# Attention and two mixtures of experts on one core: VectorE, TensorE and a fourth row buffer take over small steps at the start of the routed experts

## The chip, the cores and the metric

The kernel runs on one core of a Trainium2 chip. The time is that of one execution on the device, in microseconds (us), and the figure of a kernel is the median of several executions. One execution is also recorded by the hardware profiler; its rows are what this text reads. TensorE is called PE in the rows (PEld is its loading of weights), VectorE is DVE, ScalarE is ACT, GpSimd is POOL, and SP is the queue from which most transfers are issued.

## The reference

Three layers follow each other. First attention in chunks of 32 positions (batch 4, 8 heads, 768 positions, 64 columns a head), where each chunk also looks at 8 memory rows. Then a soft mixture of 8 experts with 4 slots each. Then a mixture of 8 experts in which every row goes to the 2 experts with the largest noisy logits:

```
scores = scale * q_c @ concat(mem_k, k_ctx).T      # per chunk of 32
x = softmax(scores) @ concat(mem_v, v_ctx)         # 3072 rows of 512
d, c = softmax(x @ phi, axis=0), softmax(x @ phi, axis=1)
x = c @ [relu((d.T @ x)[e] @ w1[e]) @ w2[e] for e in range(8)]
noisy = x @ w_gate + log1p(exp(x @ w_noise)) * noise
top2 = the two largest of noisy in each row, weights = softmax of the two
out[r] += weight * (relu(x[r] @ w1[e]) @ w2[e])    # for both experts e of row r
```

There are 3072 rows, the inner width of every expert is 1024, and the two weight matrices of one expert are 2 MB each.

## The kernel before, in words

The order of the work on each engine is the order of the program text; nothing is reordered. Each engine takes its own instructions strictly in that order and waits where an operand isn't ready.

`attention` runs over 32 half units (a pair of heads and half a sequence). In each, `qk` makes scores in PSUM: three matrix products of 128 query columns against the 16 memory columns (line 1063), then twelve of 32 query columns each against the chunk's keys, four of them side by side in the column groups of the array (line 1070). `spread` (line 1035) copies the values that `load_v` brings. `soft` then streams the 16 weight matrices of the soft experts.

`experts` does the routed experts. Its rows are sorted by expert into tiles of 128 rows, 48 tiles in the usual case and one of leftovers; the first six tiles belong to expert 0 ("rank 0"), whose weights are loaded first. A tile goes through `gather` (GpSimd fetches 128 rows from a table in memory by the indices `idx`), `ct` (TensorE turns them), `l1` (first layer on TensorE, line 707; ScalarE takes the positive part into fp16, line 709, and `lo` on VectorE takes what that lost, line 717), `l2` (24 matrix products, line 741: high part times high weights, high part times low weights, low part times high weights), `gate` and `yv` (ScalarE scales the row into a buffer `y`, line 759) and `put` (two accumulating scatters from GpSimd, line 772).

Before the first tile of an expert, its weights are prepared. `prep_g` folds the soft layer's output into the first matrix; `prep_gmax` and `prep_max` (line 374) or `bound` (ScalarE, line 449) find the largest magnitudes; `prep_row` and `prep_all` spread the maximum over the partitions by two small TensorE transpositions with a VectorE maximum between them (lines 385 to 391), for ranks 1 to 7. For rank 0 `prep_par` does that on GpSimd in one instruction (line 381). `prep_s` makes the scales, `prep_hi` (ScalarE, line 427) and `prep_lo` (VectorE, line 431) split the second matrix, in four parts, into a high and a low fp16 half; the fourth low part of rank 0 is made by `prep_lop` on GpSimd (lines 436 and 437).

Where each row of the sorted order comes from is found in two steps. For the first six tiles `spread_s` builds a one-hot matrix from 24 compares (six and six by VectorE, five by GpSimd on line 544, the rest by ScalarE), `inverse` multiplies it out and `finish_idx` turns the result into indices. For all the others `bases` and `positions` (lines 608 to 620 and `split_pos`, lines 530 to 532) find the rows' places, `tiles` makes two masks (VectorE on line 814, then GpSimd on line 815), `spread_s` makes 32 compares on VectorE and 16 on ScalarE, and `inverse` and `finish_idx` follow in the loop. `order0` and `order1` (to line 601) rank the experts by size.

The text before the loop orders the first six tiles by hand. The loop then goes over n, with tile n's second layer, tile n+1's first layer and tile n+2's turning in step n; `PLAN` and `MID` add the preparation of the next expert to fixed steps. For rank 1 these are `prep_row` in step 2 ahead of that step's second layer, `prep_s`, `prep_gs` and the first part of the split in step 3, and the other three parts in step 4. `tile_tables` (to line 799) runs on VectorE in step 3, and step n also copies the first matrix of tile n+2 into one of two small buffers (`gcopy`, line 696). The second `inverse` with `finish_idx` and the gathers of tiles 6 to 9 stand at the end of step 2. Row buffers `y` rotate over three.

Of the kernel before, what the change touches and what calls it, by code (L numbers as in the profile page):

```python
# [27 lines left out]
F = 1024  # L28
# [82 lines left out]
def tile_kernel(ctx, tc, q, k, v, mem_k, mem_v, phi, sw1, sw2, wg, wn, noise, mw1, mw2, cf_in, c16_in, out):  # L111
# [12 lines left out]
    with ExitStack() as sctx:  # L124
# [48 lines left out]
        nc.gpsimd.dma_start(nz, noise.rearrange("(t p) e -> p t e", p=128))  # L173
        C = mid.tile([128, NT, SL], F32, name="C")
        CT = mid.tile([128, 6, 128], F32, name="CT")
        SOT = mid.tile([128, 4, SL], F32, name="SOT")
# [28 lines left out]
    with ExitStack() as ectx:  # L205
        rt = ectx.enter_context(tc.tile_pool(name="rt", bufs=1))
        ew = ectx.enter_context(tc.tile_pool(name="ew", bufs=2))
        ps = ectx.enter_context(tc.tile_pool(name="ps3", bufs=1, space=PSUM))
        experts(tc, nc, C, CT, SOT, sog, wgn, nz, zt, table, mw1, mw2, out, K, K16, rw, rt, ew, ps)

# [95 lines left out]

def experts(tc, nc, C, CT, SOT, sog, wgn, nz, zt, table, mw1, mw2, out, K, K16, rw, rt, ew, ps):
    idx = rt.tile([128, NSL], I32, name="idx")
# [70 lines left out]

    def prep_par(rk, a=0, b=2):  # L380
        nc.gpsimd.partition_all_reduce(sc[:, rk, 2 + a:2 + b], sc[:, rk, a:b], 128, bass.bass_isa.ReduceOp.absmax)

    def prep_row(rk):
# [9 lines left out]
    def prep_s(rk, a=0, b=2):  # L393
        ga = sc[:, rk, 2:4]
        src = RW.get((rk, "b"), ga)
        for x in range(a, b):
            ts(ga[:, x:x + 1], src[:, x:x + 1], (2.0 ** -10, 2.0 ** -13)[x], 1.0e-34, op0=OP.mult, op1=OP.max)
        gi = ga[:, a:b].bitcast(I32)
        ts(gi, gi, 0x7F800000, None, op0=OP.bitwise_and)
        nc.vector.reciprocal(sc[:, rk, 4 + a:4 + b], ga[:, a:b])  # L400
# [28 lines left out]
    def prep_lo(rk, part):  # L429
        w2, hi, lo = w2p(rk, part)  # L430
        stt(lo, w2, sc[:, rk, 5:6], hi, op0=OP.mult, op1=OP.subtract)  # L431

    def prep_lop(rk, part):
        w2, hi, lo = w2p(rk, part)
        t = W2r[:, 7 * 4096 + 3072:8 * 4096]
        nc.gpsimd.tensor_tensor(t, w2, bc(sc[:, rk, 5:6], 1024), OP.mult)
        nc.gpsimd.tensor_tensor(lo, t, hi, OP.subtract)

# [75 lines left out]
    vt(sc[:, 0, 1:2], s4[:, :4], AX.X, OP.max)  # L514
    prep_par(0)
    cc = T(2, dt=F16)
    nc.vector.tensor_copy(cc[:96], pc)
    pp = ps.tile([128, 192], F32, name="l1", bufs=2)
    for c in range(2):
        nc.tensor.matmul(pp, cc[:96, c:c + 1].to_broadcast([96, 128]), K16["m"][:96, 192 * c:192 * c + 192],  # L520
                         start=c == 0, stop=False)
    nc.tensor.matmul(pp, K16["u"], ohb, start=False, stop=True)
    ppe = pp.rearrange("p (t e) -> p t e", e=E)
    val0 = T(NT)
# [159 lines left out]
    GT = {}  # L684
    gbuf = [x.rearrange("p a b -> p (a b)").bitcast(F16)[:, :F] for x in (C, CT)]

# [67 lines left out]

    YV = {}

    def yv(i):
        YV[i] = ew.tile([128, DM], F32, name="y", bufs=3)
        nc.scalar.activation(YV[i], P2.pop(i), AF.Copy, scale=GW.pop(i))  # L759
# [74 lines left out]
    prep_hi(0, 2)  # L834
    bases()
    ns, tq = positions()
    gcopy(0)
# [9 lines left out]
    ts(gw0, gw0, sc[:, 0, 6:7], 2.0 ** -10, op0=OP.mult, op1=OP.mult)  # L847
    prep_lop(0, 3)
    wide_w()
    tiles(0)  # L850
    prep_lo(0, 0)
    tiles(1)
    l2(0, (0,), 2)
    l1(1, False)
    l2(0, (1,), 2)
    lo(1)
    prep_lo(0, 1)
    prep_lo(0, 2)
    load_e(1, 1)
    nc.sync.dma_start(table[0:N, 64:ROW].rearrange("(t p) c -> p t c", p=128), wd)  # L860
    spread_s(oh_s, ns, J2[0], J2[1], J2[2][:16])
    l2(1, (0, 1), 2)
    prep_g(1)
    ct(2)
    l2(0, (2,), 2)
    l1(2)
    gate(0)
    yv(0)
    spread_s(oh_s, ns, [], [], J2[2][16:])
    prep_max(1, 0, 2)  # L870
    bound(2)
    ct(3)
    bound(3)
    join_max(1)
    put(0)
    PLAN, MID = {}, {}
# [31 lines left out]
    for n, i in enumerate(seq):  # L908
# [28 lines left out]
        if n == 1:  # L937
            put(i)
        if n == 2:
            inverse(oh_s, o2, [*J2[2], *J2[1], *J2[0]], T0, NSL)  # L940
            pv2 = T(NSL - T0)
            nc.scalar.activation(pv2, pvs[T0], AF.Copy)
            pvs[T0] = pv2
            finish_idx(T0, NSL)
            for x in range(6, 9):
                gather(x)
            put(i)
            gather(9)
        if n > 2:
            put(i)  # L950
# [15 lines left out]
def attention(tc, nc, q, k, v, mem_k, mem_v, phi, xs, L, K, phis, arena, ab, wk, ps, load_piece):  # L966
# [89 lines left out]
    def qk(i):  # L1056
# [4 lines left out]
        for g in range(3):  # L1061
            t = 128 * (3 * s + g)
            nc.tensor.matmul(st[:, g, :, 28:32], QT[u][:, t:t + 128], MK[:, hp, b].rearrange("p h z m -> p (h z) m"),  # L1063
                             start=True, stop=True)
        for g in range(3):
            for j in range(4):
                c = 12 * s + 4 * g + j
                w0 = 8 if c == 0 else 0
                w1 = 24 if c == NCH - 1 else 28
                nc.tensor.matmul(st[32 * j:32 * j + 32, g, :, w0:w1], QT[u][:, 32 * c:32 * c + 32],  # L1070
                                 kb[:, :, 16 * c + w0:16 * c + w1], start=True, stop=True,
                                 tile_position=(0, 32 * j))
# [295 lines left out]
```

## Time and profile before

| what | value |
|---|---|
| time, median of three executions | 607.39 us (605.48 to 607.93) |
| the profiled execution: its time | 604.92 us |
| the profiled execution: its span, first to last instruction | 603.1 us |
| granted TensorE clock, mean over the span | 0.935 |
| busy: PE, DVE, ACT, POOL | 512.6, 331.2, 292.0, 290.0 us |
| transfers | 127.28 MB, mean 211 GB/s |

Some 1.8 us of the profiled time lie outside its span. Attention takes the span's first 175 us or so, the soft experts the stretch to 230 us, the start of the routed experts that to 315 us, and from there to 583 us TensorE runs tile after tile; what is left is the last scatters. A busy share is a mean over these stages, so what a change is worth has to be read from the stage in which it lies.

### The profile page before, as it was taken

The numbers are of one execution on the slowest core, as the hardware profiler recorded it, in microseconds if no ns is written. First come the engines' busy times: TensorE is split into PE (matmuls) and PEld (weight loads), VectorE is DVE, ScalarE is ACT, GpSimd is POOL, SyncE is SP. The second block draws the span as 40 slices with busy tenths as digits, with TensorE's granted clock in tenths as the row PEclk, the third lists the DMA queues.
The fourth block names the chain that finished last, engine by engine and source line by source line (L and its number), as shares of the span: only waits on it lengthen the run. The fifth ranks groups of instructions, "written<-read, shape, count | busy, mean of one in ns | idle before, by whom it ended". The sixth has DMA issues, their size and how long they took to land.

```text
span 603.1 us, 14142 instructions
## 1 busy us (share of the span) xinstructions
PE 512.6 (85%) x4859; PEld 294.6 (49%) x4859; DVE 331.2 (55%) x826; ACT 292.0 (48%) x510; POOL 290.0 (48%) x261
## 2 busy tenths in 40 slices
PE   3998798889888866266789989999999999999960
PEld 3886686766644323132344544544545455544520
DVE  5476667565774104499486574756647566352200
ACT  4798788877531203453372452635436272452310
POOL 6032223222003000386375766757767777877762
PEclk9999999999699978568799989999999999999995
DMA  9899999999999999955749698787978867546552
GB/s 183 204 223 210 215 226 266 229 221 261 226 404 363 413 411 355 323 173 145 176 86 293 135 241 230 179 209 160 248 218 215 215 151 191 81 84 103 85 65 26
DMA packets 99505, 127.28 MB, mean 211 GB/s; under 512 B 19238, under 2 KB 68026, under 8 KB 99434
## 3 DMA queue, kind: packets, MB, share of 16 engines
q1 hardware_dynamic: 79866, 109.30, 61.0%
q0 software_dynamic: 19152, 16.89, 20.9%
q8 instruction: 45, 0.74, 0.5%
q10 hardware_dynamic: 416, 0.15, 0.1%
q14 instruction: 26, 0.21, 0.1%
HBM read 94.84 MB, written 20.42 MB: 191 GB/s over the span
## 4 chain that ended last, share of the span: by engine, by line
PE 38%; DVE 5%; DMA 5%; issue 4%; ACT 2%; POOL 2%; SPq 0%; POOLq 0%; DVEq 0%; ACTq 0%
PE l L741 31%; DMA out_dram<-y,idx 3%; PE l L707 3%; PE g L362 2%; POOL out_dram L772 1%; DMA C<-G 1%; PE l L738 1%; ACT hi L709 1%; DVE lo L717 1%; DVE mxp L374 1%; DMA w<-in_moe_w_dram 1%; ACT W L427 1%; DVE G L414 1%; DVE W L814 1%; DVE W L431 0%
## 5 line engine op out<-in xcount | busy, mean ns | idle before, releaser
L772 POOL DMA_INDIRECT out_dram<-y,idx x96 | 155.0, 1614 | 78.8 <-DMA out_dram<-y,idx 40.5
L741 PE MATMUL l<-W,hi 128*128 (+1 forms) x768 | 180.1, 389 | 0.3 <-ACT hi L709 0.3
L717 DVE SCALAR_TENSOR_TENSOR lo<-l,hi 128x1024 f16<-128x1024 f32 x49 | 59.9, 1223 | 105.3 <-ACT hi L709 73.5
L741 PEld LDWEIGHTS <-hi 128*128 128x128 f16 x768 | 74.6, 100 | 86.1 <-issue 9.6
L759 ACT ACTIVATE y<-l,gw 128x512 f32<-128x512 f32 x49 | 33.5, 684 | 148.9 <-PE l L741 87.3
L741 PE MATMUL l<-W,lo 128*128 (+1 forms) x384 | 91.9, 383 | 5.5 <-DVE lo L717 5.5
L1024 POOL DMA_DIRECT2D arena<-in_mem_v_dram x64 | 39.3, 615 | 110.4 <-PE av L1113 86.9
L666 POOL DMA_INDIRECT cg<-table,idx x49 | 52.9, 1079 | 20.4 <-issue 13.4
L741 PEld LDWEIGHTS <-lo 128*128 128x128 f16 x384 | 37.1, 98 | 50.0 <-DVE lo L717 6.2
L709 ACT ACTIVATE hi<-l 128x1024 f16<-128x1024 f32 x49 | 50.2, 1024 | 10.2 <-PE l L707 8.7
L431 DVE SCALAR_TENSOR_TENSOR W<-w,sc,W 128x1024 f16<-128x1024 f32 x31 | 42.3, 1391 | 0.2
L1035 DVE COPY arena<-arena 32x768 f32<-32x768 f32 x32 | 17.8, 555 | 39.2 <-DMA arena<-in_v_dram 34.5
L1045 PE MATMUL tr<-cf,arena 128*128 128x128 f32 x192 | 32.0, 310 | 7.0 <-DMA arena<-in_q_dram 7.0
L1052 ACT ACTIVATE qT<-tr 64x384 f32<-64x384 f32 x64 | 33.3, 520 | 6.9 <-PE tr L1045 5.8
L427 ACT ACTIVATE W<-w,sc 128x1024 f16<-128x1024 f32 x32 | 35.7, 1149 | 0.2
L1052 ACT ACTIVATE arena<-tr 64x384 f32<-64x384 f32 x64 | 30.9, 483 | 4.9 <-PE tr L1045 4.1
L1113 PE MATMUL av<-arena,aT 128*32 128x130 f32 x768 | 30.1, 291 | 2.4 <-ACT aT L1104 2.1
L1070 PE MATMUL st<-arena,qT 128*32 128x112 f32 (+2 forms) x768 | 28.2, 282 | 4.7 <-ACT arena L1052 3.9
L1045 PEld LDWEIGHTS tr<-cf,arena 128*128 128x128 f32 x192 | 23.5, 156 | 12.7 <-issue 6.9
L374 DVE TENSOR_REDUCE mxp<-w 128x1 f32<-128x2048 f32 x13 | 29.6, 2275 | 0.0
L1063 PEld LDWEIGHTS st<-arena,qT 128*128 128x128 f32 x192 | 27.3, 214 | 2.2 <-issue 2.2
L1063 PE MATMUL st<-arena,qT 128*128 128x16 f32 x192 | 26.7, 266 | 1.5 <-issue 1.5
(270 smaller groups left out, 683.6 us busy)
## 6 DMA issues: line engine op xcount, KB each, us to landing
w<-in_moe_w_dram SPq DMA_DIRECT2D x88, 512.0 KB
arena<-in_moe_w_dram SPq DMA_DIRECT2D x28, 512.0 KB
arena<-in_v_dram SPq DMA_DIRECT2D x62, 168.0 KB
arena<-in_q_dram SPq DMA_DIRECT2D x16, 384.0 KB
arena<-in_k_dram SPq DMA_DIRECT2D x16, 384.0 KB
xs<-in_moe_w_dram SPq DMA_DIRECT2D x12, 512.0 KB
out_dram<-zt SPq DMA_DIRECT2D x14, 384.0 KB
C<-G SPq DMA_DIRECT2D x21, 256.0 KB
```

The costliest lines, as they stand in the source:

```text
L374: vt(t, w2[:, part * n:(part + 1) * n], AX.X, OP.max, apply_absolute_value=True)
L427: nc.scalar.activation(hi, w2, AF.Copy, scale=sc[:, rk, 5:6])
L431: stt(lo, w2, sc[:, rk, 5:6], hi, op0=OP.mult, op1=OP.subtract)
L666: nc.gpsimd.indirect_dma_start(out=CG[i], out_offset=None, in_=table, in_offset=bass.IndirectOffsetOnAxis(ap=idx[:, i:i + 1], axis=0))
L709: nc.scalar.activation(HI[i], p, AF.Relu)
L717: stt(LO[i].rearrange("p k t -> p (k t)"), p.rearrange("p k t -> p (k t)"), 0.0, HI[i].rearrange("p k t -> p (k t)"), op0=OP.max, op1=OP.s ...
L741: nc.tensor.matmul(P2[i], h[i][:, k, :], dyn(W2f, i, w * 4096 + 512 * k, 512, RG.get(i)), start=x == 0 and k == 0, stop=x == last and k == 7)
L772: nc.gpsimd.indirect_dma_start(out=o, out_offset=bass.IndirectOffsetOnAxis(ap=idx[:, i:i + 1], axis=0), in_=y[:, DH * h:DH * h + DH], in_o ...
L1024: nc.gpsimd.dma_start(vcols(i, p + 28, 4, col, 128), bass.AP(tensor=mem_v.tensor, offset=mem_v.offset + (b * H + 2 * hp + h) * NMEM * D, a ...
L1045: nc.tensor.transpose(p[:, T, :], src[:, h, T, :], identf)
L1052: nc.scalar.activation(o, i, AF.Copy)
L1063: nc.tensor.matmul(st[:, g, :, 28:32], QT[u][:, t:t + 128], MK[:, hp, b].rearrange("p h z m -> p (h z) m"), start=True, stop=True)
```

## The change

Five things are altered. `prep_par` is taken away, and rank 0 uses `prep_row` and `prep_all` like the other ranks. `prep_lop` is taken away, and all four low parts of rank 0 are made by VectorE: two right after `order1`, the other two among the low parts of tiles 0 and 1; `bases` and `positions` move behind them. The rest of the hand-written order is changed with that: `tiles`, rank 1's `prep_g` and the compares come after tile 2's first layer, `put(0)` comes earlier, and the second `inverse`, with its indices and the gathers of tiles 6 to 9, moves from the end of step 2 to the end of step 3. In attention, the memory's scores are made by twelve products of 32 query columns in the four column groups in place of three of 128. Last, the two tiles `C` and `CT` become one tile `CC`; the two small first-matrix buffers use its first two thirds, and the last third is a fourth row buffer.

```diff
@@ attention, qk
         for g in range(3):
-            t = 128 * (3 * s + g)
-            nc.tensor.matmul(st[:, g, :, 28:32], QT[u][:, t:t + 128], MK[:, hp, b].rearrange("p h z m -> p (h z) m"),
-                             start=True, stop=True)
-        for g in range(3):
+            for j in range(4):
+                c = 12 * s + 4 * g + j
+                nc.tensor.matmul(st[32 * j:32 * j + 32, g, :, 28:32], QT[u][:, 32 * c:32 * c + 32],
+                                 MK[:, hp, b].rearrange("p h z m -> p (h z) m"), start=True, stop=True,
+                                 tile_position=(0, 32 * j))
             for j in range(4):
@@ experts, maxima of rank 0
-    def prep_par(rk, a=0, b=2):
-        nc.gpsimd.partition_all_reduce(sc[:, rk, 2 + a:2 + b], sc[:, rk, a:b], 128, bass.bass_isa.ReduceOp.absmax)
...
     vt(sc[:, 0, 1:2], s4[:, :4], AX.X, OP.max)
-    prep_par(0)
     cc = T(2, dt=F16)
     nc.vector.tensor_copy(cc[:96], pc)
+    prep_row(0)
     pp = ps.tile([128, 192], F32, name="l1", bufs=2)
...
     nc.tensor.matmul(pp, K16["u"], ohb, start=False, stop=True)
+    prep_all(0)
@@ experts, buffers
-    gbuf = [x.rearrange("p a b -> p (a b)").bitcast(F16)[:, :F] for x in (C, CT)]
+    gbuf = [CC[:, x * F // 2:(x + 1) * F // 2].bitcast(F16) for x in range(2)]
...
-        YV[i] = ew.tile([128, DM], F32, name="y", bufs=3)
+        YV[i] = CC[:, F:F + DM] if YN[0] % 4 == 3 else ew.tile([128, DM], F32, name="y", bufs=3)
+        YN[0] += 1
@@ experts, the order ahead of the loop
     ct(0)
     prep_hi(0, 2)
-    bases()
-    ns, tq = positions()
+    prep_lo(0, 0)
+    prep_lo(0, 1)
...
     ts(gw0, gw0, sc[:, 0, 6:7], 2.0 ** -10, op0=OP.mult, op1=OP.mult)
-    prep_lop(0, 3)
-    wide_w()
-    tiles(0)
-    prep_lo(0, 0)
-    tiles(1)
     l2(0, (0,), 2)
     l1(1, False)
     l2(0, (1,), 2)
+    prep_lo(0, 2)
     lo(1)
-    prep_lo(0, 1)
-    prep_lo(0, 2)
+    prep_lo(0, 3)
     load_e(1, 1)
+    bases()
+    ns, tq = positions()
+    wide_w()
     nc.sync.dma_start(table[0:N, 64:ROW].rearrange("(t p) c -> p t c", p=128), wd)
-    spread_s(oh_s, ns, J2[0], J2[1], J2[2][:16])
-    l2(1, (0, 1), 2)
-    prep_g(1)
-    ct(2)
     l2(0, (2,), 2)
-    l1(2)
     gate(0)
     yv(0)
+    put(0)
+    ct(2)
+    l2(1, (0, 1), 2)
+    l1(2)
+    tiles(0)
+    tiles(1)
+    prep_g(1)
+    spread_s(oh_s, ns, J2[0], J2[1], J2[2][:16])
+    ct(3)
     spread_s(oh_s, ns, [], [], J2[2][16:])
     prep_max(1, 0, 2)
     bound(2)
-    ct(3)
     bound(3)
     join_max(1)
-    put(0)
@@ experts, the loop
-        if n == 2:
+        if n == 3:
             inverse(oh_s, o2, [*J2[2], *J2[1], *J2[0]], T0, NSL)
...
-        if n > 2:
+        elif n > 1:
             put(i)
```

## Rows read from the trace of the kernel before

**Rows 1.** The page's chain that ended last: shares of the span by engine.

```profile
PE 38%; DVE 5%; DMA 5%; issue 4%; ACT 2%; POOL 2%; SPq 0%; POOLq 0%; DVEq 0%; ACTq 0%
```

**Rows 2.** Stretches: from:to, length, busy us by engine (instructions), PE clock, DMA share, GB/s.

```profile
80.00:120.00 40.00, 36.23 (x604) 28.84 (x600) 26.12 (x70) 33.56 (x62) 10.39 (x18) 1.00 1.08 242
...
290.00:297.00 7.00, 6.41 (x17) 2.21 (x17) 1.78 (x6) 0.00 (x0) 2.36 (x2) 0.55 0.89 273
...
520.00:580.00 60.00, 59.89 (x344) 29.77 (x343) 22.90 (x56) 24.46 (x39) 45.49 (x32) 1.00 0.51 83
```

**Rows 3.** Timeline from 241 to 260 us: start, us, engine, line, operation [idle before].

```profile
241.81 0.37 POOL L381 PARTITION_ALL_REDUCE sc<-sc  x1 [11.40 <-DVE W L517]
...
242.71 0.18 DVE L531 SCALAR_TENSOR_TENSOR W<-W,l 128x24 f32<-128x24 f32 x1
...
245.08 1.05 DVE L546 TENSOR_SCALAR W<-c,W 128x128 f16<-128x128 f16 x6
...
249.91 2.93 POOL L544 TENSOR_SCALAR W<-c,W 128x128 f16<-128x128 f16 x5 [7.73 <-DMA out_dram<-zt]
...
259.91 0.39 DVE L601 CAST eid<-W 128x8 int32<-128x8 f32 x1
```

**Rows 4.** Timeline, 263 to 281 us (and 347): VectorE and GpSimd side by side.

```profile
263.92 2.63 DVE L531 SCALAR_TENSOR_TENSOR W<-W 128x48 f32<-128x48 f32 x1
...
268.62 0.56 DVE L847 TENSOR_SCALAR gw<-gw,sc 128x6 f32<-128x6 f32 x1
268.64 0.52 POOL L632 TENSOR_TENSOR W<-W 128x192 f32<-128x192 f32 x1
269.09 1.54 DVE L814 TENSOR_TENSOR W<-c,W 128x1344 f16<-128x1344 f16 x1
...
275.02 2.32 DVE L431 SCALAR_TENSOR_TENSOR W<-w,sc,W 128x1024 f16<-128x1024 f32 x1
...
275.02 5.70 DVE L431 SCALAR_TENSOR_TENSOR W<-w,sc,W 128x1024 f16<-128x1024 f32 x2
276.22 3.41 POOL L815 TENSOR_TENSOR W<-W,cfb 128x1344 f16<-128x1344 f16 x1
...
347.22 2.48 DVE L431 SCALAR_TENSOR_TENSOR W<-w,sc,W 128x1024 f16<-128x1024 f32 x2
```

**Rows 5.** Timeline: the first gather, then TensorE's path into the loop.

```profile
255.10 1.48 POOL L666 DMA_INDIRECT cg<-table,idx  x1 [2.26 <-issue]
...
259.02 0.29 PE L671 MATMUL ct<-c,cg 128*128 128x128 f16 x1 [5.70 <-DMA cg<-table,idx]
...
290.59 0.37 PE L385 MATMUL g<-cf,sc 128*2 128x128 f32 x1 [3.03 <-DVE sc L807]
...
298.91 1.40 PE L649 MATMUL ct<-W 128*128 128x56 f16 x48
...
300.67 0.61 PE L707 MATMUL l<-ctt,G 128*128 128x128 f16 x8
...
306.80 3.62 PE L741 MATMUL l<-W,hi 128*128 128x512 f16 x16
...
312.93 0.16 DVE L799 TENSOR_TENSOR tmE<-cfb,W 128x16 f32<-128x16 f32 x1
...
314.59 0.62 PE L707 MATMUL l<-ctt,C 128*128 128x128 f16 x8 [2.40 <-DMA C<-G]
```

**Rows 6.** Timeline: one half unit of attention, the two kinds of score products.

```profile
82.44 0.74 PE L1063 MATMUL st<-arena,qT 128*128 128x16 f32 x6
...
83.11 0.78 PE L1070 MATMUL st<-arena,qT 128*32 128x112 f32 x24
```

**Rows 7.** Waits of the whole span: engine, line <- awaited: us, times, longest.

```profile
DVE arena L1035 <- DMA arena<-in_v_dram: 34.5, 21, 3.9
```

**Rows 8.** The page's groups: out<-in, count | busy, mean ns | idle before.

```profile
L717 DVE SCALAR_TENSOR_TENSOR lo<-l,hi 128x1024 f16<-128x1024 f32 x49 | 59.9, 1223 | 105.3 <-ACT hi L709 73.5
...
L374 DVE TENSOR_REDUCE mxp<-w 128x1 f32<-128x2048 f32 x13 | 29.6, 2275 | 0.0
```

More of the change, by code (lines that the diff above doesn't have):

```diff
@@ L173, in tile_kernel @@
         nc.gpsimd.dma_start(nz, noise.rearrange("(t p) e -> p t e", p=128))
-        C = mid.tile([128, NT, SL], F32, name="C")
-        CT = mid.tile([128, 6, 128], F32, name="CT")
+        CC = mid.tile([128, 2 * NT * SL], F32, name="CC")
+        C = CC[:, :NT * SL].rearrange("p (t s) -> p t s", s=SL)
+        CT = CC[:, NT * SL:].rearrange("p (t n) -> p t n", n=128)
         SOT = mid.tile([128, 4, SL], F32, name="SOT")
@@ L208, in tile_kernel @@
         ps = ectx.enter_context(tc.tile_pool(name="ps3", bufs=1, space=PSUM))
-        experts(tc, nc, C, CT, SOT, sog, wgn, nz, zt, table, mw1, mw2, out, K, K16, rw, rt, ew, ps)
+        experts(tc, nc, CC, CT, SOT, sog, wgn, nz, zt, table, mw1, mw2, out, K, K16, rw, rt, ew, ps)
 def zero_out(q, out, zt, a, b):
@@ L304, in soft, with experts @@
     nc.vector.tensor_copy(SOT, pt)
-def experts(tc, nc, C, CT, SOT, sog, wgn, nz, zt, table, mw1, mw2, out, K, K16, rw, rt, ew, ps):
+def experts(tc, nc, CC, CT, SOT, sog, wgn, nz, zt, table, mw1, mw2, out, K, K16, rw, rt, ew, ps):
     idx = rt.tile([128, NSL], I32, name="idx")
@@ L394, in prep_s @@
         ga = sc[:, rk, 2:4]
-        src = RW.get((rk, "b"), ga)
+        src = RW[rk, "b"]
         for x in range(a, b):
@@ L431, in prep_lo @@
         stt(lo, w2, sc[:, rk, 5:6], hi, op0=OP.mult, op1=OP.subtract)
[L433 to L437, printed above, removed]
     s4 = T(5)
@@ L755, in experts @@
     YV = {}
+    YN = [0]
     def yv(i):
-        YV[i] = ew.tile([128, DM], F32, name="y", bufs=3)
+        YV[i] = CC[:, F:F + DM] if YN[0] % 4 == 3 else ew.tile([128, DM], F32, name="y", bufs=3)
+        YN[0] += 1
         nc.scalar.activation(YV[i], P2.pop(i), AF.Copy, scale=GW.pop(i))
```

## Prediction

> **What bounds the kernel now.** I read the chain of waits first. TensorE holds 38% of the span and no other engine more than 5% [rows 1], and the chain can't be followed back past about 250 us, so the time is set from there on. The stretches say why there are two halves. Until 230 us the transfers are the limit: from 80 to 120 us the DMA engines are busy 1.08 of the time while TensorE has 36.23 of 40 us [rows 2], and VectorE waits 34.5 us in 21 pieces for attention's values [rows 7]. At the far end TensorE is full, 59.89 of 60 us between 520 and 580 [rows 2]. In between, from 241 to 315 us, no engine is full. There the timeline has to be read instruction by instruction, and nearly all of the change lies there.
>
> Three things are to be seen in that stretch. GpSimd makes five of the first 24 compares on line 544. Their input is ready at 242.71 + 0.18 = 242.89, yet they begin at 249.91, after an idle of 7.73 that starts right behind the `PARTITION_ALL_REDUCE` [rows 3]. The transfer that the row names as releaser is no operand of it. Second, VectorE and GpSimd hold each other up. A VectorE operation of 48 elements took 2.63 us against 0.18 for one of 24 [rows 3, 4], and of two low parts one ended at 277.34, the other at 280.72, which is 1.09 after GpSimd's mask had ended at 279.63 [rows 4]; alone two take 2.48 [rows 4]. So one waits until the other's operation is over, and the mask itself needs 279.63 - 277.34 = 2.3 us. Third, TensorE waited 3.03 us at 290.59 for rank 1's maximum, and then ran at a granted clock of 0.55 until 297, partly at 1.2 GHz, where 17 instructions took 6.41 us [rows 2, 5].
>
> **The change, part by part.** Times are in the profiled execution.
>
> A. The reduction leaves GpSimd, and with it the idle behind it. VectorE pays for it: a TensorE turn of 0.37 as on line 385 [rows 5] and a small maximum stand ahead of the positions, about 0.4 us. VectorE's last six compares end at 246.13 + 0.4 in place of GpSimd's last at 252.84 [rows 3], so the first indices come 252.84 - 246.53 = 6.3 us earlier, and `order1` ends at 254.0 instead of 260.30 [rows 3]. The price is bounded by 0, if GpSimd's first compare pays anyway, and by 6.3; I take 6.3, because the row ahead of the idle is the one removed. The Trainium skill, GPSIMD Engine Reference, section 2.1 Instruction dispatch, says that the first call to a freshly loaded GpSimd kernel pays about 6 us without a visible instruction; this trace shows 7.0 from the operand to the start, and with the page's 5.95 the gain would be 5.3 and the forecast 1 us higher.
>
> B. In the place of `bases` and `positions` come two low parts. From 254.0: two low parts 2.48, tile 0's low half 1.22 [rows 8], gate scales about 0.8 (an estimate, four operations near 0.2 as line 531 in rows 3), a third part 1.24, about 1 us of waiting for tile 1's first layer (an estimate), its low half 1.22, the fourth part 1.24: 263.2. Then `bases` and `positions` without the hold, 263.92 + 0.18 - 260.30 = 3.8 us [rows 3, 4]: 267.0. Before they ended near 266.7. The 6.3 us are spent: the fourth part came from GpSimd beside other work, and the parts now stand ahead of the positions instead of behind them.
>
> C. `tiles` stands behind tile 2's low half on VectorE, and that behind TensorE. After 263.2 TensorE needs a last piece of tile 0 (0.45), tile 1's 16 products (3.62), a first layer (0.61) [rows 5], ScalarE's pass 1.2 (an estimate, like a low part), and VectorE's low half 1.22: 270.4. VectorE idles some 2 us. If TensorE is still at 1.2 GHz here, the 16 products cost up to twice that, 3.6 us more.
>
> D. Two masks on VectorE at 1.5 (1.54, line 814) give 273.4. GpSimd's two mask operations follow, 2.3 each, while VectorE's 32 compares are due. Before, the compares came after them. Whether a compare is held by a mask no row shows. It is bounded by 0 and by 4.6 us; the nearest row is another TENSOR_SCALAR, line 847, which took 0.56 instead of about 0.2 and ended at 269.18, with GpSimd's line 632 ending at 269.16 [rows 4]. I take held: 278.0, then 31 compares at 1.05 / 6 = 0.175 [rows 3], rank 1's maximum 2.28 [rows 8] and 0.4 of joining: 286.1. Before, the turn of that maximum was at 290.59 [rows 5], so it comes 4.5 us earlier; unheld 282.1, 8.5 earlier. The Trainium skill, SBUF — State Buffer, section Who interferes with whom, gives a rule that speaks against this order: a `tensor_scalar` can enter a mode that takes the port pair shared with GpSimd, and whoever issues first keeps it for the whole instruction. By it the compares are held and the sum stands; without it rival 1 below holds.
>
> E. From that turn to tile 6's first layer, before: 314.59 - 290.59 = 24.0 us. After, the second `inverse` comes one step later. To tile 4's first layer: 300.67 - 290.59 = 10.1, less the inverse (1.40) and its hand-over (0.3) = 8.4. From there VectorE runs tile 4's low half, rank 1's scales and split and all of `tile_tables`, to 313.09: 12.4 us [rows 5]. Before, the second indices were made ahead of this list; now they stand behind it, because `tile_tables` comes first in step 3. Four small operations follow, 1.1 with the hand-over (an estimate as in B), then the gather of tile 6: 1.5 if only its issue counts, 259.02 - 255.10 = 3.9 by the first gather, which met full DMA engines [rows 5]; I take 2.5. So tile 6 can be turned 24.4 us after the maximum. TensorE has by then done tile 4's first layer, step 3 (5.4) and the inverse, about 16 us, and stands idle for 8.5, since the turn of tile 6 is ahead of tile 5 in its order. Then turn, first layer, step 4's 24 products and a turn: 0.2 + 0.6 + 5.4 + 0.2 = 6.4 at full clock [rows 5]; behind an idle I take 16 products at 6.41 / 17 = 0.38 [rows 2] and 8 at 0.23: 8.9 in place of 6.4. In all 24.4 + 8.9 = 33.3, against 24.0: 9.3 us later. The 2.40 us that tile 6 waited for its matrix copy [rows 5] are hidden inside this.
>
> F. Moves that cost nothing. GpSimd's `put(0)` now stands ahead of the masks, but it is through by about 269; the masks start at 273. ScalarE's 16 compares and tile 3's turn behind them end near 277, covered by VectorE's list to 286. The table write waits on `wide_w` and on SP behind `load_e(1, 1)`, whose last piece is free at 263 instead of 281; it has 40 us to land. If the list on VectorE were shorter by 9 us, these would come next.
>
> G. The column groups. Six products of the wide kind took 0.74, 24 narrow ones with seven times the moving columns 0.78 [rows 6]. In each of 32 half units the new ones cost between nothing and 0.78, so the change is -0.74 to +0.04; I take -0.2, near to line 1070, which has their number and form, 6.4 us in all. Nearly all of it turns into longer waiting for the values [rows 7]; for the stretches in which transfers are not the limit I count -0.6.
>
> H. The fourth row buffer lets ScalarE go on earlier when scatters are late. TensorE is full there [rows 2], so 0.
>
> The sum: -4.5 + 9.3 - 0.6 = +4.2 us; from tile 6 on everything follows TensorE, scatters included. Against the profiled 604.92 that is 609.1; the median, 607.39, lies 2.5 above it, so 611.6. The bounds of A (none) stand as rival 4. The others give, for held compares, -4.5 + 6.8 - 0.6 = +1.7 (full clock in E) to -0.9 + 9.3 + 1.4 - 0.6 = +9.2 (half clock in C, slow gather): 609.1 to 616.6.
>
> **The rivals.** 1. The compares aren't held by the masks. Then -8.5 + 9.3 - 0.6 = +0.2, or -2.3 at full clock: 605.1 to 607.6, the middle 606.4. For it: line 847 is one row, of another type. Against it: the low parts and that row behave alike. This one is not slower, and it decides as soon as the 32 compares start while GpSimd works.
>
> 2. TensorE and ScalarE, not transfers, pace attention. Then the 6.4 us of G count in full: 607.39 + 4.8 - 6.4 = 605.8. For it: TensorE is busy 36.23 of 40 us; against it the DMA share of 1.08 [rows 2] and the waits [rows 7].
>
> 3. Both at once: 607.39 + 0.8 - 6.4 = 601.8, or some 2 us less at full clock; faster.
>
> 4. GpSimd's first compare pays the idle even without the reduction, for instance because the transfers of that moment are the reason. Then A's 6.3 fall away and all of it is later: 617.9.
>
> **How the numbers follow.** Forecast 0.47, rival 1 0.18, rival 2 0.11, rival 3 0.08, rival 4 0.08, anything else 0.08, evenly to both sides. The range that leaves out 2 in 10 goes from 602.5 to 617. A measurement here tells 0.5%, about 3 us, from no change: 604.4 to 610.4. Faster: rival 3, a part of rivals 1 and 2 and half the rest, 0.2. Within: most of rivals 1 and 2 and the low end of the forecast, 0.3. Slower: 0.5.
>
> **What would show it.** Right: no gap ahead of line 544; a gap of VectorE's compares as long as GpSimd's masks; the maximum's turn near 286; second indices right behind `tile_tables`; TensorE idle 8 us ahead of tile 6's turn and a low clock after it. Wrong: compares that run beside the masks, attention ending more than 2 us earlier, or indices that don't wait for `tile_tables`.

## The result, and the profile after

The changed kernel takes 612.49 us in the median (609.04 to 621.37, 20 executions), the kernel before, run beside it, 607.47 (600.64 to 615.79, 20 executions). The ratio is 1.0102, with a 95% interval from 1.007 to 1.0133; this ratio and those below leave out slow executions, more than 1.5% above the fastest of their kernel, and the traces of runs 1, 3 and 7 are of such executions. So the change is slower by 5.0 us by the medians and by 6.2 by the ratio; 611.6, 4.2 us above 607.39, was forecast. The profiled execution of after has a span of 611.7 us; busy times first, then the chain that ended last, by engine:

```profile
span 611.7 us, 15292 instructions
PE 502.9 (82%) x5437; PEld 278.9 (46%) x5437; DVE 332.4 (54%) x828; ACT 292.0 (48%) x510; POOL 284.7 (47%) x258
...
PE 37%; DVE 7%; DMA 5%; issue 4%; POOL 3%; ACT 2%; another core or an unknown queue 0%; SPq 0%; POOLq 0%; DVEq 0%; ACTq 0%
```

VectorE's share of that chain has gone from 5% [rows 1] to 7%. The stretch of after from the turn of rank 1's maximum to tile 6's first layer (columns as in rows 2):

```profile
287.20:320.00 32.80, 23.07 (x144) 11.18 (x145) 15.95 (x37) 10.15 (x17) 13.30 (x10) 0.77 0.32 65
```

TensorE is busy for 23.07 of 32.8 us at a granted clock of 0.77. The stretch with the same work took 24.0 us before [rows 5]. The timelines show where that comes from. GpSimd first (start, duration, engine, line, operation, out<-in, count, idle before and its releaser):

```profile
242.71 3.34 POOL L537 TENSOR_SCALAR W<-c,W 128x128 f16<-128x128 f16 x5 [13.83 <-DVE W L525]
...
273.33 6.08 POOL L810 TENSOR_TENSOR W<-W,cfb 128x1344 f16<-128x1344 f16 x2 [3.34 <-DVE W L809]
...
308.87 1.01 POOL L659 DMA_INDIRECT cg<-table,idx  x1 [1.32 <-DVE idx L653]
```

The five compares that started at 249.91 after an idle of 7.73 [rows 3] now start at 242.71, the moment VectorE's operation delivers. VectorE:

```profile
253.09 0.38 DVE L594 CAST eid<-W 128x8 int32<-128x8 f32 x1
253.38 2.73 DVE L429 SCALAR_TENSOR_TENSOR W<-w,sc,W 128x1024 f16<-128x1024 f32 x2
...
268.58 0.17 DVE L525 TENSOR_SCALAR W<-W 128x48 f32<-128x48 f32 x1
270.55 1.22 DVE L710 SCALAR_TENSOR_TENSOR lo<-l,hi 128x1024 f16<-128x1024 f32 x1 [1.80 <-ACT hi L702]
271.69 3.02 DVE L809 TENSOR_TENSOR W<-c,W 128x1344 f16<-128x1344 f16 x2
...
274.96 9.53 DVE L539 TENSOR_SCALAR W<-c,W 128x128 f16<-128x128 f16 x32
...
304.02 0.16 DVE L777 TENSOR_TENSOR W<-W 128x8 f32<-128x8 f32 x1
...
307.67 0.17 DVE L794 TENSOR_TENSOR tmE<-cfb,W 128x16 f32<-128x16 f32 x1
...
308.38 0.22 DVE L653 SCALAR_TENSOR_TENSOR idx<-W 128x56 int32<-128x56 f32 x1
```

`order1` ends at 253.47, the positions (line 525) at 268.75. The 32 compares (line 539) take 9.53 us while GpSimd makes its masks, from 273.33 to 279.41. Taken one by one, the first two compares last 2.10 and 2.48 us and end at 277.06 and 279.46; GpSimd's two masks last 3.68 and 2.44 and end at 277.01 and 279.41. The second indices (lines 650 to 653) stand right behind the tables (lines 777 to 794). TensorE:

```profile
287.18 0.37 PE L383 MATMUL g<-cf,sc 128*2 128x128 f32 x1 [8.72 <-DVE sc L802]
287.35 6.09 PE L734 MATMUL l<-W,hi 128*128 128x512 f16 x16
...
300.93 1.40 PE L642 MATMUL ct<-W 128*128 128x56 f16 x48
312.07 0.29 PE L664 MATMUL ct<-c,cg 128*128 128x128 f16 x1 [9.73 <-DMA cg<-table,idx]
...
313.00 5.22 PE L734 MATMUL l<-W,hi 128*128 128x512 f16 x16
...
319.84 0.61 PE L700 MATMUL l<-ctt,CC 128*128 128x128 f16 x8
```

Tile 6's turn at 312.07, ahead of tile 5's first layer in TensorE's order, waits 9.73 us for the gathered rows, and the 16 products behind each long idle take 6.09 and 5.22 us in place of 3.62 [rows 5]. Tile 6's first layer comes at 319.84, 5.25 us later than before [rows 5], though attention ended 1.53 us earlier in this trace.

### The profile page after: what moved, and what is told of

The parts are those of the page before. It is cut to its first block, busy times and chain, and to the rows that moved or that the text cites. A ratio compares the mean times of both kernels' runs of the same rounds, so it can differ in the third digit from the quotient of the medians.

```text
span 611.7 us, 15292 instructions
## 1 busy us (share of the span) xinstructions
PE 502.9 (82%) x5437; PEld 278.9 (46%) x5437; DVE 332.4 (54%) x828; ACT 292.0 (48%) x510; POOL 284.7 (47%) x258
## 4 chain that ended last, share of the span: by engine, by line
PE 37%; DVE 7%; DMA 5%; issue 4%; POOL 3%; ACT 2%; another core or an unknown queue 0%; SPq 0%; POOLq 0%; DVEq 0%; ACTq 0%
PE l L734 31%; PE l L700 3%; DMA out_dram<-y,idx 3%; POOL out_dram L767 2%; DVE W L539 2%; PE g L363 2%; DVE lo L710 1%; ACT hi L702 1%; DMA cg<-table,idx 1%; DVE W L429 1%; PE l L731 1%; DVE G L412 1%; DVE mxp L375 1%; DMA CC<-G 1%; DMA out_dram<-CC,idx 1%
## 5 line engine op out<-in xcount | busy, mean ns | idle before, releaser
L767 POOL DMA_INDIRECT out_dram<-y,idx x72 | 116.7, 1620 | 71.6 <-ACT ctt L666 27.6
L734 PE MATMUL l<-W,lo 128*128 (+1 forms) x384 | 91.1, 380 | 0.0
L754 ACT ACTIVATE y<-l,gw 128x512 f32<-128x512 f32 x37 | 25.3, 683 | 123.9 <-PE l L734 106.6
L659 POOL DMA_INDIRECT cg<-table,idx x49 | 55.0, 1122 | 17.7 <-issue 12.0
L767 POOL DMA_INDIRECT out_dram<-CC,idx x24 | 38.2, 1590 | 21.0 <-DMA out_dram<-y,idx 11.2
L1066 PE MATMUL st<-arena,qT 128*32 128x112 f32 (+2 forms) x768 | 33.0, 278 | 14.2 <-ACT arena L1047 7.3
L429 DVE SCALAR_TENSOR_TENSOR W<-w,sc,W 128x1024 f16<-128x1024 f32 x32 | 40.4, 1287 | 0.2
L1059 PE MATMUL st<-arena,qT 128*32 128x16 f32 x768 | 26.7, 190 | 4.9 <-issue 4.9
```

The costliest lines, as they stand in the source:

```text
L659: nc.gpsimd.indirect_dma_start(out=CG[i], out_offset=None, in_=table, in_offset=bass.IndirectOffsetOnAxis(ap=idx[:, i:i + 1], axis=0))
L734: nc.tensor.matmul(P2[i], h[i][:, k, :], dyn(W2f, i, w * 4096 + 512 * k, 512, RG.get(i)), start=x == 0 and k == 0, stop=x == last and k == 7)
L767: nc.gpsimd.indirect_dma_start(out=o, out_offset=bass.IndirectOffsetOnAxis(ap=idx[:, i:i + 1], axis=0), in_=y[:, DH * h:DH * h + DH], in_o ...
```

## The experiments

Four times are read from each trace. "Attention's end" is the start of ScalarE's copy of the soft layer's last output projection, at 230.19 in the trace of before; turn (of rank 1's maximum) and tile 6 (its first layer) are counted from it. "41 to 43" is the time between first layers number 41 and 43, counted from 0, five and seven behind that of the leftovers (which runs 6 and 8 move eight places ahead); two steps of a full TensorE are 11.37. All in us; a ratio is to the kernel before in the same session, with its 95% interval.

| kernel | attention's end | turn | tile 6 | 41 to 43 | span | ratio |
|---|---|---|---|---|---|---|
| before | 230.19 | 60.4 | 84.4 | 11.37 | 603.1 | 1 |
| before, second trace (12) | 224.93 | 59.8 | 82.6 | 15.95 | 603.1 | |
| after | 228.66 | 58.5 | 91.2 | 13.21 | 611.7 | 1.0102 [1.007, 1.0133] |
| 1 before, reduction replaced | 232.41 | 56.1 | 80.2 | 17.35 | 609.1 | 0.992 [0.9875, 0.9966] |
| 2 after, inverse in step 2 | 227.27 | 57.3 | 80.6 | 18.77 | 601.1 | 1.001 [0.9962, 1.0058] |
| 3 after, compares first | 230.97 | 55.2 | 86.5 | 18.63 | 614.3 | 1.0015 [0.9955, 1.0076] |
| 4 before, column groups | 229.06 | 60.3 | 84.1 | 18.16 | 608.7 | 1.0046 [0.9999, 1.0093] |
| 5 after, three row buffers | 228.64 | 57.9 | 91.1 | 12.60 | 609.7 | 1.0081 [1.0028, 1.0135] |
| 6 before, leftovers early | 225.06 | 60.4 | 84.6 | 11.37 | 605.2 | 1.0006 [0.9965, 1.0046] |
| 7 both orders (2 and 3) | 233.79 | 56.1 | 79.4 | 18.89 | 610.4 | 0.9934 [0.9881, 0.9987] |
| 8 as 7, with another far end | 228.98 | 55.5 | 78.2 | 11.37 | 603.4 | 1.0028 [0.998, 1.0076] |
| 9 after, tables last | 229.22 | 57.5 | 85.7 | 18.95 | 607.8 | 1.0056 [1.0012, 1.01] |
| 10 before, two of eight scatters | 226.65 | 60.5 | 83.1 | 11.36 | 593.2 | 0.9885 [0.9825, 0.9944] |
| 11 as 2, maximum ahead of masks | 229.62 | 49.9 | 73.7 | 19.29 | 599.9 | 0.9876 [0.9816, 0.9936] |

A single trace is one execution, and the two of the unchanged kernel differ by 5.3 us at attention's end; so mechanisms are read from the columns counted from there, and times from the ratios. The expectations of runs 7 and 11 give tile 5's first layer as 82 to 83 us from attention's end; these were read from a zero 10.5 us too early, and 72.4 is meant. The differences in them hold.

**1. The reduction alone (part A in the kernel before).**

```diff
-    prep_par(0)
...
+    prep_row(0)
...
+    prep_all(0)
```

> The kernel before, with part A alone: the absolute maximum over the partitions is taken by a TensorE turn and a small VectorE maximum in place of GpSimd's PARTITION_ALL_REDUCE. Theory (the reduction causes the idle ahead of GpSimd's first compares): no gap ahead of those compares, the gathers' order ends near 254 us in place of 260.3, and as VectorE is busy 29.33 of 30 us from 260 to 290, most of the 6.3 us reach the end: 601 to 603 us. Rival (GpSimd's first compare pays the idle whatever stands ahead of it): gap of about 7 us stays, 607.5 us. Second rival (the gain is given back at the next weights from memory, on which the chain of before stands for 4.20 us at 262): no gap, but 605 to 607 us.

```profile
246.55 3.34 POOL L545 TENSOR_SCALAR W<-c,W 128x128 f16<-128x128 f16 x5 [13.93 <-DVE W L533]
...
243.60 2.94 POOL L544 TENSOR_SCALAR W<-c,W 128x128 f16<-128x128 f16 x5 [6.95 <-issue]
```

(The second row is from the second trace of before, run 12.) The compares start 246.55 - 232.41 = 14.1 us after attention's end, where before they needed 249.91 - 230.19 = 19.7, or 243.60 - 224.93 = 18.7 in the second trace; there the idle of 6.95 behind the reduction names no transfer. The idle was the reduction's, rival 4 falls, and the ratio of 0.992 (4.9 us) is as the theory had it. The gain at the compares is 5.6 us by the first trace of before and 4.5 by the second, and 4.2 or 2.4 of it reach tile 6.

**2. The second inverse back in step 2 (step E undone).**

```diff
-        if n == 3:
+        if n == 2:
             inverse(oh_s, o2, [*J2[2], *J2[1], *J2[0]], T0, NSL)
```

> The kernel after, with the second inverse, the second indices and the gathers of tiles 6 to 9 back at the end of step 2, so ahead of the tables of tiles on VectorE. Theory (step E: these indices queued behind the tables cost the 8.7 us between rank 1's maximum and tile 6's first layer): TensorE's 9.73 us idle ahead of tile 6's turn is gone, tile 6's first layer comes 22 to 25 us after the turn of rank 1's maximum in place of 32.7, and the time is 602 to 605 us. Rival (tile 6 waits for its matrix copy or for weights anyway, so that only a part comes back): idle stays at 4 us or more, 608 to 611 us.

```profile
284.55 0.37 PE L383 MATMUL g<-cf,sc 128*2 128x128 f32 x1 [9.19 <-DVE sc L802]
...
292.26 1.40 PE L642 MATMUL ct<-W 128*128 128x56 f16 x48
...
299.64 0.22 PE L664 MATMUL ct<-c,cg 128*128 128x128 f16 x1
...
307.83 0.62 PE L700 MATMUL l<-ctt,CC 128*128 128x128 f16 x8 [2.29 <-DMA CC<-G]
```

The idle ahead of tile 6's turn (299.64) is gone, and tile 6 comes 307.83 - 284.55 = 23.3 us behind the maximum's turn, as the theory said; a wait of 2.29 us for tile 6's matrix copy has come back. Counted from attention's end tile 6 is 10.6 us earlier than in after, but the ratio only 0.009 lower, 5.6 us (2 to 9, an estimate from the two intervals): the mechanism is the theory's, the time, 608.1 (605.2 to 611.0), is the rival's. The same trace has a loss at the far end: first layer 43 comes 18.77 us behind number 41, in after 13.21.

```profile
536.27 0.29 PE L664 MATMUL ct<-c,cg 128*128 128x128 f16 x1 [4.29 <-DMA cg<-table,idx]
...
517.71 1.38 POOL L762 DMA_INDIRECT out_dram<-y,qidx  x1 [0.30 <-issue]
...
532.06 1.32 POOL L762 DMA_INDIRECT out_dram<-y,qidx  x1 [0.30 <-issue]
533.69 1.01 POOL L659 DMA_INDIRECT cg<-table,idx  x1 [0.30 <-issue]
```

(TensorE's row first, then GpSimd's.) It waits 4.29 us for a gather that GpSimd issues at 533.69, behind the eight scatters of the leftovers' tile (line 762). This is not the whole account: from attention's end to the end of the span this trace is 9.2 us shorter than that of after, so the two traces by themselves don't show where the difference between 10.6 and 5.6 went.

**3. The compares ahead of the masks (step D).**

```diff
-    tiles(0)
-    tiles(1)
     prep_g(1)
     spread_s(oh_s, ns, J2[0], J2[1], J2[2][:16])
     ct(3)
     spread_s(oh_s, ns, [], [], J2[2][16:])
+    tiles(0)
+    tiles(1)
     prep_max(1, 0, 2)
```

> The kernel after, with rank 1's 32 compares on VectorE ahead of the two masks, so that GpSimd's two mask operations of 3 us fall beside VectorE's masks and maximum and not beside the compares. Theory (step D: a mask on GpSimd holds the compares): the 32 compares take 5.3 to 5.8 us in place of 9.53, the turn of rank 1's maximum comes 3 to 5 us earlier than 287.2, and the time is 607.5 to 609.5 us. Rival (the compares are slow for another reason, or the maximum is held in their place): the turn within 1 us of 287.2, time 611.5 to 613.

```profile
273.18 5.29 DVE L539 TENSOR_SCALAR W<-c,W 128x128 f16<-128x128 f16 x32
278.38 3.02 DVE L809 TENSOR_TENSOR W<-c,W 128x1344 f16<-128x1344 f16 x2
281.31 2.28 DVE L375 TENSOR_REDUCE mxp<-w 128x1 f32<-128x2048 f32 x1
...
283.88 2.23 DVE L802 TENSOR_TENSOR sc<-sc,mxp 128x1 f32<-128x1 f32 x1
...
280.02 6.07 POOL L810 TENSOR_TENSOR W<-W,cfb 128x1344 f16<-128x1344 f16 x2 [8.87 <-DVE W L809]
```

The compares take 5.29 us, 4.24 less. But GpSimd's masks, now from 280.02 to 286.09, hold something else: the joining of the maximum, one column on line 802, took 2.23 us in place of 0.16 and ended at 286.11. So 2.07 of the 4.24 us were lost again; the turn came 3.3 us earlier, of which 1.1 arose elsewhere. The maximum itself (2.28) and the copy behind it ran beside the masks without loss. The ratio of 1.0015 is 608.4 us, within what the theory expected, but its interval, 604.7 to 612.1, reaches into the rival's range: it is the rows that decide.

**4. The column groups alone (part G).** The diff of `qk` in the kernel before, nothing else.

> The kernel before, with part G alone: the scores of the memory slots in four column groups of 32 in place of one wide product. Theory (step G: the transfers pace attention, and the products gain little): 606.5 to 607.5 us, attention's end less than 1 us earlier. Rival (TensorE and ScalarE pace attention, so that the products' gain counts in all 32 half units): 600.5 to 603 us. Third case (narrow products cost more in all): 608 us.

The score products of both kinds taken together (busy time of PE, PEld and DVE on tile `st` from 0 to 175 us; the other columns as in rows 2), first in before, then in this run:

```profile
0.00:175.00 175.00, 53.37 (x960) 46.70 (x960) 38.21 (x96) 0.96 1.02 233
...
0.00:175.00 175.00, 37.48 (x1536) 27.47 (x1536) 38.21 (x96) 0.94 1.03 236
```

TensorE was busy with them for 53.37 us before (51.34 in the second trace), 37.48 now. By their own line the memory's products show no gain, 26.7 us for 192 and 26.2 for 768. But in the new form they alternate with the context's products, four and four, and run beside them, so the two lines' times overlap and can't be added. In a half unit without a wait inside, the time from the first score product to the next operation is 83.82 - 82.44 = 1.38 us before and 66.99 - 66.09 = 0.90 in this run: 0.48 saved, some 15 us in 32 half units. TensorE's whole busy time up to 175 us falls from 149.1 to 138.7 us, yet attention's end lies between 224.93 and 232.41 in the five traces with the old form and between 227.27 and 233.79 in the nine with the new. So TensorE doesn't pace attention, and rival 2 falls. The DMA engines' share stays at 1.02 and 1.03; whether ScalarE holds attention back beside the transfers this run can't tell. The ratio of 1.0046 (610.3 us) is above the forecast's own figure, and why it isn't below 1 stays open.

**5. Three row buffers (part H undone).**

```diff
-        YV[i] = CC[:, F:F + DM] if YN[0] % 4 == 3 else ew.tile([128, DM], F32, name="y", bufs=3)
-        YN[0] += 1
+        YV[i] = ew.tile([128, DM], F32, name="y", bufs=3)
```

> The kernel after, with part H undone: three buffers for the weighted rows in place of four, all else as in after. Theory (step H: the fourth buffer is worth nothing as long as TensorE is full): within 2 us of 612.5. Rival (the fourth buffer lets scatters fall further behind, and the delay of 3 us that after gathers between tile 12 and the last tile comes from it): 608 to 610 us. Third case (the fourth buffer keeps ScalarE and TensorE from waiting for late scatters): 614 to 617 us.

1.0081 against 1.0102, within both intervals: the fourth buffer is worth nothing that can be measured, as forecast.

**6. The leftovers earlier**, in the kernel before.

```diff
-RB = 12
+RB = 20
```

> The kernel before, with the tile of leftovers (eight scatters of 32 rows, 13.6 to 15.7 us of GpSimd's time) 20 tiles ahead of the end in place of 12. Theory (at the far end GpSimd's chain of scatters, about 59 us from the end of the leftovers' scatters to the last one in each trace so far, sets the end, and it recovers some 0.6 us per tile against TensorE's 5.7): no TensorE stall of several us behind the leftovers, end 3 to 5 us earlier, 603 to 605 us. Rival (TensorE sets the end and the scatters only follow): within 1.5 us of the kernel before.

No gain (1.0006). The stall did not vanish, it moved with the leftovers: first layer 34 came 11.69 us behind number 33 in place of 5.68, and the end was no earlier. The theory's conclusion, that the chain recovers with more tiles behind it, is wrong; that TensorE alone sets the end, as the rival has it, isn't borne out either, by that stall and by run 10.

**7. Both orders, 2 and 3 together.**

> The kernel after, with both changes of order: second indices at the end of step 2, and rank 1's 32 compares ahead of the masks. Theory (steps D and E are separate costs): tile 5's first layer comes about 2 us earlier after attention's end than with the first change of order alone (82.9 us after the last output projection's copy), time 601 to 604 us. Rival (GpSimd's masks, now 6 us later, hold VectorE elsewhere or delay the inverse): tile 5 within 0.7 us of 82.9, time as with the first change alone.

Tile 5 comes 71.3 us after attention's end, 1.1 earlier than in run 2: between theory and rival, since the joining is still held. The ratio, 0.9934, is 603.5 us.

**8. Another far end on top of run 7.**

```diff
-RB = 12
+RB = 20
-        if n > 3 and n + 6 < len(seq):
-            gather(seq[n + 6])
...
+            if n > 2:
+                for x in range(n + 6 if n == 3 else n + 7, n + 8):
+                    if x < len(seq) and x > 9:
+                        gather(seq[x])
             put(i)
```

> The same kernel with both changes of order, and at the far end the tile of leftovers 20 tiles ahead of the end and each gather one tile further ahead, in front of the scatters of its step. Theory (GpSimd's scatters set the end): 4 to 7 us faster than with the two orders alone, 595 to 599 us. Rival (TensorE sets it): within 1.5 us of the kernel with the two orders alone.

1.0028 against 0.9934: not the 4 to 7 us faster that the theory had. Whether it is slower than run 7 isn't shown: the intervals touch, and in the single traces the span ends 374.4 us after attention's end, in run 7 376.6. As in run 6 the stall moved with the leftovers: first layer 35 came 9.83 us behind number 34. Why the earlier gathers don't help stays open.

**9. The tables behind the second indices, still in step 3.**

```diff
-        if n == 3:
-            tile_tables()
...
             put(i)
             gather(9)
+            tile_tables()
```

> The kernel after, with the tables of tiles behind the second indices and the gathers of step 3; the second inverse stays at the end of step 3. It splits step E: the tables alone take 3.8 us on VectorE (302.57 to 306.39 in the run with the inverse in step 2). Theory (the indices wait for everything that step 3 puts on VectorE, the tables being the last piece of it): the gather of tile 6 about 3.8 us earlier, TensorE's idle ahead of tile 6's turn near 6 us in place of 9.7, and part of that given back at tile 6's matrix copy, which needs the tables: 608 to 611 us. Rival (the tables alone are the cause, as the prediction put it in its first sentence on them): the idle falls below 2 us and the time to 604 us.

```profile
299.97 1.41 PE L642 MATMUL ct<-W 128*128 128x56 f16 x48
306.98 0.29 PE L664 MATMUL ct<-c,cg 128*128 128x128 f16 x1 [5.61 <-DMA cg<-table,idx]
```

The idle falls from 9.73 to 5.61 us, by 4.1, and the ratio of 1.0056 is 610.9 us, both as the theory had it. The tables are about half of the delay, 4.1 of 9.7 us by the idle and 5.5 of run 2's 10.6 by tile 6's first layer; the rest is what step 3 gives VectorE besides, up to the first low part of rank 1.

**10. Two of the leftovers' eight scatters.**

```diff
-            for q in range(4):
+            for q in range(1):
```

> The kernel before; of the eight scatters of the leftovers' tile only the first two are issued, so that the rows of its other three groups are missing from the output. Six scatters and their spacing are about 11 us of GpSimd's chain. Theory (GpSimd's chain of scatters sets the end): 4 to 8 us faster than the kernel before, no TensorE wait for a gathered tile of several us near 540, and the last scatters right behind their rows. Rival (TensorE sets the end, and the chain has slack): within 1.5 us of the kernel before.

The time falls by 1.15% (7.0 us), 41 to 43 is 11.36, and the trace has no wait for a gathered tile. The last rows leave ScalarE and are scattered at once:

```profile
579.62 0.69 ACT L759 ACTIVATE y<-l,gw 128x512 f32<-128x512 f32 x1 [4.54 <-PE l L741]
...
580.58 1.54 POOL L772 DMA_INDIRECT out_dram<-y,idx  x1 [1.85 <-ACT y L759]
582.42 1.54 POOL L772 DMA_INDIRECT out_dram<-y,idx  x1 [0.30 <-issue]
```

In before they are not: the last row is ready at 584.19, and its scatters go at 589.17 and 591.36.

```profile
583.50 0.69 ACT L759 ACTIVATE y<-l,gw 128x512 f32<-128x512 f32 x1 [4.54 <-PE l L741]
...
589.17 1.54 POOL L772 DMA_INDIRECT out_dram<-y,idx  x1 [0.33 <-issue]
591.36 1.54 POOL L772 DMA_INDIRECT out_dram<-y,idx  x1 [0.65 <-DMA out_dram<-y,idx]
```

In after it is the same, 593.45 for the row and 600.27 for the last scatter. The chain that ended last says so too. In this run it stays with TensorE until 579.54; in before it leaves TensorE at 555.57 and goes through GpSimd's gathers and scatters, and from 561.96 on mostly through the landing of scatters, 3.4 to 5.1 us at a time.

**11. As run 2, and the maximum and its joining ahead of the masks.**

```diff
     spread_s(oh_s, ns, [], [], J2[2][16:])
     prep_max(1, 0, 2)
     bound(2)
     bound(3)
     join_max(1)
+    tiles(0)
+    tiles(1)
```

> The kernel after, with the second indices at the end of step 2, and on VectorE rank 1's compares, its maximum and the joining all ahead of the two masks, so that no VectorE operation on the way to the maximum's turn stands beside a GpSimd mask. Theory (step D: masks on GpSimd hold VectorE's small operations, 4.2 us of compares or 2.1 us of the joining): the turn comes 50 to 52 us after the last output projection's copy in place of 57.3 with the first change alone and 56.0 with both; tile 5's first layer 3 to 5 us earlier than 82 us if the masks are then in time for the second inverse. Time 600 to 603 us. Rival (the masks become late, or the scatters at the far end eat the gain): turn as said, but tile 5 within 1 us of 82, 603 to 605 us.

```profile
271.54 5.29 DVE L539 TENSOR_SCALAR W<-c,W 128x128 f16<-128x128 f16 x32
276.74 2.28 DVE L375 TENSOR_REDUCE mxp<-w 128x1 f32<-128x2048 f32 x1
...
279.30 0.16 DVE L802 TENSOR_TENSOR sc<-sc,mxp 128x1 f32<-128x1 f32 x1
279.38 3.02 DVE L809 TENSOR_TENSOR W<-c,W 128x1344 f16<-128x1344 f16 x2
282.31 1.22 DVE L710 SCALAR_TENSOR_TENSOR lo<-l,hi 128x1024 f16<-128x1024 f32 x1
...
281.01 6.07 POOL L810 TENSOR_TENSOR W<-W,cfb 128x1344 f16<-128x1344 f16 x2 [11.52 <-DVE W L809]
...
279.52 0.37 PE L383 MATMUL g<-cf,sc 128*2 128x128 f32 x1 [1.68 <-DVE sc L802]
...
303.31 0.62 PE L700 MATMUL l<-ctt,CC 128*128 128x128 f16 x8 [2.84 <-DMA CC<-G]
```

No operation on the way to the turn is held; the turn is at 49.9, tile 5 at 65.0, 7.4 us ahead of run 2 where 3 to 5 were expected, and tile 6 at 73.7, 6.9 ahead. At 0.9876 (7.5 us) it has the lowest ratio of the kernels with all their work (the intervals of runs 1 and 7 overlap with it) and is faster than both before and after, although 41 to 43 took 19.29, 7.9 more than with a full TensorE.

**12. The kernel before once more**, unchanged.

> The kernel before, unchanged, in a second profiled execution: how much of the differences between single traces is the execution's own. If the first trace of it was an ordinary one, attention ends (last output projection's copy) within 0.5 us of 230.19, tile 43's first layer comes 11.4 us after tile 41's, and the span is 603 us. If the scatters' chain varies by itself, attention's end differs by 1 to 4 us, and tile 43 comes 12 to 20 us after tile 41 with a wait for a gathered tile, as in five of the changed kernels; span 605 to 610 us.

Attention ended 5.3 us earlier than in the first trace, more than either case had, tile 6 by 7.05, and the span is the same 603.1: what was won there was lost again, 4.6 us of it between first layers 41 and 43. TensorE's longest wait between 500 and 600 us (in total, times, longest) is one that the first trace doesn't have:

```profile
PE ct L671 <- DMA cg<-table,idx: 2.1, 1, 2.1
```

## Why the forecast held, step by step

The time (612.49 for 611.6) and the direction were right, and the largest term, E, was right by its mechanism and near in size. But the gain ahead of it was less than half of what was forecast, the column groups were mis-sized, one assumption was wrong, and that the time came out so close is in part luck.

A. Right in kind, smaller in size: 5.6 us at GpSimd's compares in run 1 (4.5 by the second trace of before) against 6.3. The Trainium skill, GPSIMD Engine Reference, section 2.1 Instruction dispatch, gives about 6 us for the first call to a freshly loaded kernel, by which 5.3 were to be won; the run's two figures lie on either side of that, and that a kernel is loaded there isn't shown.

B. The parts ahead of the positions took 268.75 - 253.47 = 15.3 us up to the end of the positions, where 13.0 were forecast. The two estimates, 0.8 for the gate scales and 1 for waiting, were low: VectorE waited 0.70, 0.89 and 1.17 us in three places, and a gate scale took 0.56.

C. The end of tile 2's low half, 271.77 for 270.4 (its terms add up to 270.3), follows from B; the idle of VectorE was 1.80 for "some 2".

D. The compares were held, by 4.24 us (run 3) where 2 x 2.3 were taken. The price of a mask was right: GpSimd's first mask, 3.68 us long, began while VectorE's second was still running and ended 2.30 after it, the second took 2.44. Two compares were held, each until a mask was over. (Without the hold the same terms give 281.7, not 282.1, so rival 1 lies 0.4 us lower.) The maximum's turn came at 287.18, forecast 286.1. In the trace it is 3.4 us earlier than before, but attention had ended 1.53 earlier, so the kernel's own gain is 1.9 (1.3 by the second trace of before) where 4.5 were forecast: that is the term that was mis-sized, and A (0.7) and B (2.3) account for it. Rival 1, the compares not held, and rival 3 fall with run 3. The rule in the Trainium skill, SBUF — State Buffer, section Who interferes with whom, agrees with both orders here: a `tensor_scalar` of fp16 and a two-input operation on SBUF waited for GpSimd, the reduction over one input didn't.

E. From the turn to tile 6: 32.66 us, forecast 33.3. The idle ahead of tile 6's turn was 9.73 for 8.5, and 16 products behind it took 5.22 for 6.08. Runs 2 and 9 bear it out: without the queue on VectorE it is 23.3, with the tables alone out of the way 28.2.

F. No row shows a cost of a moved step.

G. Wrong in size, right that it wouldn't show: 0.48 us a half unit by run 4, some 15 in all, where 0.2 and 6.4 were taken, and attention ended no earlier. That any of it reaches the end, the 0.6 us of the sum, no run shows. The 1.5 us by which attention ended earlier in after is less than the 5.3 between two traces of one kernel.

H. 0, as forecast (run 5).

What was wrong is the sentence that from tile 6 on everything follows TensorE, scatters included. GpSimd falls behind at the leftovers' eight scatters, TensorE then waits for gathers queued behind them, and the last scatters come late: taking six of the eight away gave 7.0 us (run 10), and tile 6 earlier by 10.6 us gave 5.6 (run 2). The trace of before had shown it: its chain leaves TensorE at 555.57, though TensorE is full from 520 to 580 [rows 2].

Here luck comes in. Counted from attention's end the change delayed tile 6 by 6.8 us against the first trace of before and by 8.6 against the second, where -4.5 + 9.3 = 4.8 were forecast; the time moved by 5.0 (6.2 by the ratio). What lies between tile 6's first layer and the end of the span took 288.5 and 295.5 us in the two traces of before and 291.9 in that of after, so it is no constant to which a delay at tile 6 is added. What the far end decides is what a cure is worth. How much is lost there changes from trace to trace, 0 and 4.6 us in 41 to 43 in the two of before and up to 7.9 in the others, and what sets that isn't settled: GpSimd's waits for scatters to land vary in the same traces, but no run changed them alone.

## What to carry to other kernels

Taking a stall away is worth what the steps behind it leave of it: here some 5 us were won at GpSimd and lost by putting a list of table building ahead of the indices that TensorE waits for, so each moved instruction is to be costed by who queues behind it on its own engine. Work for GpSimd that reads SBUF belongs beside VectorE's reductions or its PSUM reads, not beside its compares or its two-input operations. Before a gain at the front is counted in full, see whether another engine's queue at the far end, here the scatters, has slack of its own: follow the chain that ended last back from its end, and don't take a full TensorE for the limit. And where two kinds of products run side by side, read their common busy time, not that of each line.

## What the runs showed of the hardware

A one-column operation with two inputs in SBUF took 2.23 us beside a GpSimd mask, in place of 0.16, while a reduction of 2048 columns kept its 2.28 and low halves read from PSUM their 1.22 (runs 3 and 11). The hold goes both ways: GpSimd's mask took 3.68 us where it began beside a VectorE mask, ending 2.30 after that one, and 2.44 where it didn't (after). Splitting three products with 128 query columns into twelve with 32, in four column groups and alternating with the context's products, brought the scores of a half unit from 1.38 to 0.90 us, and TensorE's busy time in attention down by some 10 us; attention, with the DMA engines' share at 1.02 and 1.03, ended no earlier (run 4). Behind idles of 8.72 and 9.73 us 16 products took 6.09 and 5.22 us where 3.62 is usual, in a stretch with a mean granted clock of 0.77, so partly at 1.2 and partly at 2.4 GHz. One kernel's attention ended at 224.93 in one execution and at 230.19 in another.
